# A linear-attention and spectral-mixing kernel: VectorE's table preparation moved ahead of the row work, TensorE's part spread among the rows, and one zeroing moved from VectorE to GpSimd

## The chip, the cores and the metric

The kernel runs on one core of one Trainium2 chip. The metric is the device time of one execution in microseconds (us); the figure for the kernel before is the median of three runs. The profile comes from one more execution, whose own time is given beside its span (first to last instruction). The engines are TensorE (PE in the profile; its weight loads are PEld), VectorE (DVE), ScalarE (ACT), GpSimd (POOL) and SyncE (SP); 16 DMA engines move data between HBM and the on-chip memory.

## The reference

Linear attention over 8 batches, 8 heads, 576 positions and head size 64, then a mixing step in the frequency domain: a real FFT along the sequence, a complex 512 x 512 product for each of the 64 lowest modes, the inverse FFT added to the input, and a channel product with a rectifier.

```python
def phi(x):
    return np.where(x > 0, x, np.exp(x) - 1.0) + 1.0
q_p, k_p = (phi(q), phi(k))
kv = np.einsum('bhsd,bhse->bhde', k_p, v)
z = np.sum(k_p, axis=2)
num = np.einsum('bhsd,bhde->bhse', q_p, kv)
den = np.einsum('bhsd,bhd->bhs', q_p, z)[..., None] + 1e-06
x = num / den                                # heads side by side: (8, 576, 512)
X = np.fft.rfft(x, axis=1)
Xr, Xi = np.real(X[:, :64]), np.imag(X[:, :64])
Yr = np.einsum('bmd,mde->bme', Xr, w_r) - np.einsum('bmd,mde->bme', Xi, w_i)
Yi = np.einsum('bmd,mde->bme', Xr, w_i) + np.einsum('bmd,mde->bme', Xi, w_r)
Y[:, :64] = Yr + 1j * Yi
y = np.fft.irfft(Y, n=S, axis=1)
u = x + y
return u + np.maximum(u @ w_ch, 0.0)
```

The weights w_r and w_i are 64 matrices of 512 x 512 in float32 each.

## The kernel before

**Three stages.** First, attention: for each of the 8 batches q, k and v are loaded, made into features, and summed into a k-v matrix per head (kept in kv_sb); the attention rows are formed once for the forward transform, which makes the left operands xt. Second, the spectral products: the weights are taken in 32 loads w0 to w31, each a tile of 128 x 8192 in bf16 (2 MB as stored, converted on the way from float32); an even load holds the real parts of four modes, the odd one behind it the imaginary parts. For each load, mode_block(p) runs a block of 16 matmuls of 128 x 512 (line 525) on TensorE, p being the load's number, and behind each odd block the sums are evacuated (lines 534 and 536) and sorted. The last loads go in a somewhat different way. Third, a tail behind the last load: the last sums, rectifier, additions and stores to the output.

**Order of work.** Nearly every instruction is pinned: each engine runs them in the order in which the program lists them. An instruction that waits for a semaphore therefore holds all that stand behind it on its engine.

**The weight loads.** All are issued by GpSimd (w_load, line 106) in its one queue, in order. The first two buffers (w0, w1) are kept and reused for all loads from w6 on; w2, w3 and w4 lie in a pool of their own (wpre), and w5 in a further one (wx) beside it. A load from w6 on has to wait till the block that last read its buffer is done: w6 waits for block 0, w7 for block 1, w8 for block 6, and so on. mode_block(p) places the load in the program when it takes the block up (w_get).

**The memory of w2 to w5.** After block 5 the pools of w2 to w5 are closed (line 711), and a new pool, sW, takes their place. It holds the rows x_main and x_tail, small tiles, and kv_diag: the k-v matrices laid out with zeros beside them (128 x 4160 in f16), so that one matmul serves two heads. kv_diag is zeroed (line 720) and then filled by two copies from kv_sb (line 722). What writes to sW first has to wait for the loads and blocks that used the memory before.

**The work between the blocks.** Blocks 6 and later have two slots each, "mid" and "end". A list of small functions (work) is dealt to them by share (line 1065) in given weights; work_slot runs so many of them at each slot. At the head of the list stand the attention rows, which are formed a second time for the output (attention_rows, line 821: for a tile of rows, matmuls of q features with kv_diag, then a division on VectorE into x_main or x_tail). Behind them follow the folding of inverse rows into x and the channel products.

**The inverse table and the row sets.** inverse_rows (line 757) makes the inverse transform's table inv_sb from the forward one, fwd_sb: 16 copies on VectorE sort the modes into by_mode (line 770), five matmuls transpose them (line 780), and VectorE scales the results into inv_sb (lines 782 and 788). row_sets (line 794) makes three 0-1 matrices in sel on VectorE: a memset and ten copies. row_set(i) (line 807) multiplies inv_sb by one of these on TensorE and lets ScalarE copy the result into inv2_sb or into a lead_sb. In the list these five items stand together behind the first five tiles of rows (lines 1097 to 1100); inverse_rows and row_sets have their VectorE part inside the item.

Of the kernel before, what the change touches and what calls it, by code (L numbers as in the profile page):

```python
# [11 lines left out]
F16 = mybir.dt.float16  # L12
# [21 lines left out]
def kernel(  # L34
# [10 lines left out]
    nc = tc.nc  # L45

    B, H, S, Dh = q.shape
    D = H * Dh
    NM = moe_w_r.shape[0]
    NHP = H // 2  # L50
    NDC = D // 128
# [41 lines left out]
    pin = tc.keep_in_program_order  # L93
# [52 lines left out]
    def rows_of(jj: int, base: int = 0):  # L146

        if jj < NJJ:
            return slice(base + jj, base + 512, NJJ)
        return slice(512, S) if base == 0 else slice(0, base)  # L150
# [14 lines left out]
    def q_view(t):  # L165
        return t.rearrange("p (c t s) -> p c t s", c=2, t=2)
# [508 lines left out]
    N_LEAD = 2  # L675
# [37 lines left out]
    sW = ctx.enter_context(tc.tile_pool(name="sW", bufs=1))  # L713
# [3 lines left out]
        sW.tile([128, 2, D], F32, tag="x_tail", bufs=B // 4, name=f"x_tail{i}") for i in range(B // 4)  # L717
    ]
    kv_diag = sW.tile([128, B, 2, 2, 2, 65], F16, tag="YZ", bufs=1, name="kv_diag")
    pin(nc.vector.memset(kv_diag, 0.0))  # L720
    for h in range(2):
        pin(nc.vector.tensor_copy(out=kv_diag[HALVES[h], :, :, :, h, :], in_=kv_sb[HALVES[h]]))
    yz_at: list = []
# [11 lines left out]
    def x_of(t: int):  # L735
        if t < B * NJJ:
            return x_main[t // NJJ][:, t % NJJ, :]
        i = t - B * NJJ
        return x_tail[i // 2][:, i % 2, :]
# [10 lines left out]
    def bank(name: str, shape=(128, D), dtype=F32):  # L750
        return psB.tile(list(shape), dtype, tag="bank", bufs=4, name=name)
# [2 lines left out]

    inv_scale = sW.tile([128, 1], F32, name="inv_scale")

    def inverse_rows():

        pin(nc.vector.memset(inv_scale, INV_EXP))
        pin(nc.vector.memset(inv_scale[0:2], INV_EXP / 2))  # L760
        by_mode = [
            sW.tile([128, NDC, 128], F16, tag="xTw", bufs=2, name="modes_main"),
            sW.tile([128, D], F16, tag="x16w", bufs=2, name="modes_tail")[:, 0:128].unsqueeze(1),
        ]
        for dst, src in zip(by_mode, (fwd_sb[:, 0:NJJ, :], fwd_sb[:, NJJ:, :])):
            for t in range(2):
                for g in range(4):
                    c0 = t * NM + g * NQ
                    pin(
                        nc.vector.tensor_copy(  # L770
                            out=dst[:, :, 2 * g + t :: 8], in_=src[:, :, c0 : c0 + NQ]
                        )
                    )
        iv = bank("inv_main", [128, NJJ, 128])
        it = bank("inv_tail")
        for jj in range(NJJ + 1):
            rows = slice(0, 128) if jj < NJJ else slice(0, S - 512)
            modes = by_mode[jj // NJJ][rows, jj % NJJ, :]
            o = iv[:, jj] if jj < NJJ else it[:, 0 : S - 512]
            pin(nc.tensor.matmul(o, modes, id16[rows, rows]))  # L780
        pin(
            nc.vector.tensor_scalar(
                out=inv_sb[:, 0:512].rearrange("m (p j) -> m j p", j=NJJ), in0=iv,
                scalar1=inv_scale[:, 0:1], scalar2=None, op0=ALU.mult,
            )
        )
        pin(
            nc.vector.tensor_scalar(
                out=inv_sb[:, 512:S], in0=it[:, 0 : S - 512],
                scalar1=inv_scale[:, 0:1], scalar2=None, op0=ALU.mult,  # L790
            )
        )

    def row_sets():
        pin(nc.vector.memset(sel, 0.0))
        for h in range(2):
            for g in range(NF // NL):
                r0 = 2 * NF + 2 * NL * ((g - 1) % (NF // NL))
                pin(
                    nc.vector.tensor_copy(  # L800
                        out=sel[:, 0, h * 64 + g : h * 64 + 64 : NF // NL], in_=id16[:, r0 : r0 + 2 * NL]
                    )
                )
        for b in range(N_LEAD):
            pin(nc.vector.tensor_copy(out=sel[:, 1 + b, b:128:B], in_=id16[:, 2 * NE : 128]))

    def row_set(i: int):
        dst = ([inv2_sb] + lead_sb)[i]
        for cols in (slice(0, 512), slice(512, S)):
            r_ps = bank(f"rows{i}_{cols.start}")[:, 0 : cols.stop - cols.start]  # L810
            pin(nc.tensor.matmul(r_ps, sel[:, i, :], inv_sb[:, cols]))
            pin(nc.scalar.copy(out=dst[:, cols], in_=r_ps))

    def parts_of(t: int):
        if t < B * NJJ:
            b, jj = divmod(t, NJJ)
            return [(b, jj, slice(0, 128))]
        p = t - B * NJJ
        return [(2 * p + h, NJJ, HALVES[h]) for h in range(2)]

    def attention_rows(t: int):

        num = [bank(f"nw{t}_{c}") for c in range(2)]
        x = x_of(t)
        for b, jj, orow in parts_of(t):
            qT = q_view(qT_all[b])
            rd = rd_all[b][orow, jj].rearrange("p o (c t) -> p c t o", c=2)
            xv = x[orow].rearrange("p (o c t d) -> p c t o d", o=2, c=2, t=2)
            for c in range(2):
                for h2 in range(2):  # L830
                    pin(
                        nc.tensor.matmul(  # L832
                            num[c][orow, h2 * 130 : h2 * 130 + 130],
                            qT[:, c, h2, rows_of(jj, BASE[b % 2])],
                            kv_diag[:, b, c, h2].rearrange("p o n -> p (o n)"),
                        )
                    )
            for c in range(2):
                nv = num[c][orow, 0:260].rearrange("p (t o n) -> p t o n", t=2, o=2)
                rden = rd[:, c]  # L840
                if b % 2 == 1:
                    rden = sW.tile([128, 2, 2], F32, tag="rdw", bufs=4, name=f"rdw{t}_{c}")[orow]
                    pin(nc.vector.reciprocal(out=rden, in_=nv[:, :, :, 64]))
                pin(
                    nc.vector.tensor_tensor(  # L845
                        out=xv[:, c],
                        in0=nv[:, :, :, 0:64],
                        in1=rden.unsqueeze(3).broadcast_to([orow.stop - orow.start, 2, 2, Dh]),
                        op=ALU.mult,
                    )  # L850
                )
# [18 lines left out]
    x16w, xTw = {}, {}  # L870
# [40 lines left out]
    tiles = []  # L911
# [153 lines left out]
    def share(n_items: int, steps: list):  # L1065
        total, at = sum(w for _, w in steps), 0
        for key, w in steps:
            lo = at
            at += w
            slots[key] = slots.get(key, 0) + n_items * at // total - n_items * lo // total  # L1070
# [16 lines left out]
    def first_rows(n: int):  # L1087
        for i, t in enumerate(pairs[n]):
# [5 lines left out]
                ),  # L1094
            )

    rows_work = [inverse_rows, row_sets] + [lambda i=i: row_set(i) for i in range(1 + N_LEAD)]
    work[:0] = [lambda t=t: attention_rows(t) for t in tiles[:5]] + rows_work + [
        lambda t=t: attention_rows(t) for t in tiles[5:]
    ]  # L1100
    share(
        len(tiles) + len(rows_work),
        [((p, h), 10) for p in range(n_early, first_fold - 2) for h in ("mid", "end")]
# [166 lines left out]
```

## Time and profile before

| | |
|---|---|
| median of 3 runs | 418.39 us (418.31 to 419.18) |
| the profiled execution | 419.09 us, span 417.4 us |
| busy: TensorE, VectorE, ScalarE, GpSimd | 306.6, 244.7, 148.7, 51.9 us |
| mean granted TensorE clock | 0.829 of full speed |
| DMA queue of GpSimd (weights, q, k, v) | 81.53 MB written, 94.1% of the 16 engines' span |
| weight loads of 2048 KB | 29, median 16.8 to 17.0 us from issue to landing |
| HBM read and written | 163.66 MB and 9.44 MB |

The costliest groups among those that the change touches, and the blocks:

| line, engine | work | count | mean |
|---|---|---|---|
| 525, PE | a matmul of a block, 128 x 512 | 480 | 498 ns |
| 720, DVE | zeroing kv_diag, 128 x 4160 | 1 | 3525 ns |
| 722, DVE | filling kv_diag | 2 | 698 ns |
| 704 and 469, POOL | zeroing xz, 128 x 1536 | 2 | 1397 ns |
| 106, POOL | issuing a weight load | 31 | 546 and 533 ns |

Times in the profile count from the start of the span. A row of the timeline names its start, its length, engine, line, operation, what is written and what is read, and in brackets how long the engine sat idle before it and what ended the wait. A row of the stretches gives the busy time of each engine with its instructions, then the granted clock, the share of the DMA engines' time that was busy, and the rate at which they moved data. A load's landing is its issue plus its time to landing. Idle time of an engine off the chain costs nothing by itself.

### The profile page before, as it was taken

Reading aid. Unit: us, or ns where it says so; the run is one execution under the profiler, and the core shown is the slowest. Engines: PE = TensorE matmul, PEld = TensorE weight load, DVE = VectorE, ACT = ScalarE, POOL = GpSimd, SP = SyncE. Lnnn points to the kernel's source line nnn. Section 1 sums busy time; section 2 is a strip of 40 time slices with the busy share of each in tenths; the row PEclk is TensorE's granted clock in tenths of the full one; section 3 lists DMA queues with packets and bytes.
Section 4 is the critical chain, followed back from the end, with each engine's and each line's share of the span. In section 5 each row is a group of like instructions: output and inputs, shape, how many; then the busy total and the mean of one; then the engine's idle time right before and its main releaser. Section 6 shows DMA issues by size and latency. Waiting matters only on the chain.

```text
span 417.4 us, 6710 instructions
## 1 busy us (share of the span) xinstructions
PE 306.6 (73%) x2767; PEld 173.5 (42%) x2767; DVE 244.7 (59%) x540; ACT 148.7 (36%) x220; POOL 51.9 (12%) x91
## 2 busy tenths in 40 slices
PE   0269799999685365786665568778879887887993
PEld 0167687777442132243332233333434433452431
DVE  3779979884752546566574342556445644622795
ACT  4667788854300001000000112334434442322682
POOL 6233424000110000010000000001000000230200
PEclk9999858556979565676665688999989999999998
DMA  8999999999999999999999999999999999999698
GB/s 216 211 211 217 209 219 205 221 221 216 214 220 210 220 218 210 212 216 210 218 214 221 218 210 220 217 214 220 213 221 217 212 217 218 215 210 187 210 401 346
DMA packets 16691, 92.84 MB, mean 222 GB/s; under 512 B 2069, under 2 KB 2790, under 8 KB 12374
## 3 DMA queue, kind: packets, MB, share of 16 engines
q0 software_dynamic: 12784, 81.53, 94.1%
q1 hardware_dynamic: 3878, 10.90, 6.9%
q8 instruction: 21, 0.34, 0.3%
q14 instruction: 8, 0.07, 0.0%
HBM read 163.66 MB, written 9.44 MB: 415 GB/s over the span
## 4 chain that ended last, share of the span: by engine, by line
DMA 60%; PE 22%; DVE 9%; issue 4%; ACT 2%; POOL 2%; POOLq 0%; ACTq 0%; DVEq 0%
DMA w<-in_moe_w_r_dram 34%; DMA w<-in_moe_w_i_dram 17%; PE P L525 9%; DMA k<-in_k_dram 7%; PE kvp L264 4%; DVE x_main L1031 4%; DMA q<-in_q_dram 3%; PE qTp L244 2%; DVE x L300 2%; PE xf L434 1%; ACT ke L210 1%; DVE xz L453 1%; PE eps L901 1%; PE num L158 1%; PE acc L955 1%
## 5 line engine op out<-in xcount | busy, mean ns | idle before, releaser
L525 PE MATMUL P<-w,xz 128*64 128x512 bf16 x480 | 81.1, 498 | 46.2 <-DMA w<-in_moe_w_i_dram 22.8
L525 PEld LDWEIGHTS <-xz 128*64 128x64 bf16 x480 | 38.2, 136 | 79.2 <-issue 66.6
L536 ACT CAST ys<-P 128x512 f16<-128x512 f32 x8 | 4.7, 585 | 115.8 <-PE P L525 115.8
L901 PE MATMUL eps<-wch,xTw 128*128 128x512 f16 x144 | 37.3, 383 | 3.8 <-DVE xTw L893 3.8
L882 DVE TENSOR_TENSOR x_main<-ya,x_main 128x512 f32<-128x512 f32 x32 | 21.9, 687 | 23.8 <-PE ya L878 23.7
L884 ACT CAST x16w<-x_main 128x512 f16<-128x512 f32 x32 | 19.8, 619 | 41.5 <-DVE x_main L882 40.7
L453 DVE COPY xz<-xt 32x384 bf16<-32x384 bf16 (+2 forms) x62 | 31.1, 502 | 2.1 <-ACT xt L419 1.2
L832 PE MATMUL nw<-kv_diag,qT 128*128 128x130 f16 (+1 forms) x160 | 23.1, 273 | 11.3 <-DVE x_main L845 6.4
L264 PE MATMUL kvp<-vpad,ke 32*128 32x130 f16 x576 | 24.8, 275 | 8.4 <-ACT qT L251 8.4
L909 ACT CAST E<-eps 128x512 f16<-128x512 f32 (+1 forms) x40 | 21.1, 538 | 21.5 <-PE eps L901 21.5
L264 PEld LDWEIGHTS <-ke 32*128 32x128 f16 x576 | 23.1, 123 | 9.8 <-issue 9.1
L106 POOL DMA_DIRECT2D w<-in_moe_w_i_dram x15 | 8.0, 533 | 142.4 <-PE P L525 95.4
L244 PE MATMUL qTp<-id,qe 128*128 128x128 f16 x144 | 16.8, 311 | 11.5 <-DVE qe L228 9.7
L832 PEld LDWEIGHTS <-qT 128*128 128x128 f16 (+1 forms) x160 | 14.6, 130 | 24.2 <-issue 12.2
L534 DVE CAST ys<-P 128x512 f16<-128x512 f32 x10 | 6.9, 691 | 29.6 <-PE P L525 29.6
L106 POOL DMA_DIRECT2D w<-in_moe_w_r_dram x16 | 8.7, 546 | 118.6 <-PE P L525 118.4
L893 DVE COPY xTw<-xTp 128x512 f16<-128x512 f16 x36 | 14.9, 416 | 13.7 <-PE xTp L891 13.6
L300 DVE TENSOR_TENSOR x<-num,rd 128x512 f16<-128x512 f32 x32 | 22.1, 691 | 1.1
L158 PE MATMUL num<-kv_sb,qT 64*128 64x65 f16 (+1 forms) x320 | 16.7, 226 | 6.0 <-DVE x L300 3.9
L251 ACT COPY qT<-qTp 128x1152 f16<-128x1152 f16 x16 | 19.5, 1282 | 2.9 <-PE qTp L244 2.4
L244 PEld LDWEIGHTS <-qe 128*128 128x128 f16 x144 | 14.8, 146 | 12.5 <-DVE qe L228 10.1
L901 PEld LDWEIGHTS <-xTw 128*128 128x128 f16 x144 | 12.4, 99 | 15.1 <-DVE xTw L893 4.4
(162 smaller groups left out, 498.6 us busy)
## 6 DMA issues: line engine op xcount, KB each, us to landing
w<-in_moe_w_i_dram POOLq DMA_DIRECT2D x15, 2048.0 KB, 17.0
w<-in_moe_w_r_dram POOLq DMA_DIRECT2D x14, 2048.0 KB, 16.8
out_dram<-x_main SPq DMA_DIRECT2D x14, 512.0 KB, 3.4
v<-in_v_dram POOLq DMA_DIRECT2D x8, 576.0 KB, 13.9
q<-in_q_dram POOLq DMA_DIRECT2D x7, 576.0 KB, 12.6
k<-in_k_dram POOLq DMA_DIRECT2D x6, 576.0 KB, 12.6
w<-in_moe_w_r_dram POOLq DMA_DIRECT2D x2, 1024.0 KB, 16.6
w<-in_moe_w_r_dram POOLq DMA_DIRECT2D x4, 512.0 KB, 11.8
```

The source lines that it names most:

```text
L158: mm = nc.tensor.matmul(num[hpo][orow, c0 : c0 + 65], qT[rows, hpp, h2, cols], kv_sb[rows, hpp, h2, :])
L244: nc.tensor.transpose(qT_ps[:, j], phi["q", b][:, c, j].rearrange("p o d -> p (o d)"), id16,)
L251: nc.scalar.copy(out=qT[:, :, c * NJ : (c + 1) * NJ], in_=qT_ps.rearrange("p j x -> p x j"))
L264: nc.tensor.matmul(kv_ps[:, h2, 0:130], phi["k", b][r0 : r0 + 32, j // NJ, j % NJ].rearrange("p o d -> p (o d)"), vp[r0 : r0 + 32, :, j, 0 ...
L300: nc.vector.tensor_tensor(out=dst.rearrange("p (o c d) -> p o c d", o=2, c=4), in0=nv[:, :, :, 0:64], in1=rden.unsqueeze(3).broadcast_to([ ...
L453: pin(copies[g % len(copies)](out=xz[k % 2][rows, :, :, g, of], in_=src))
L525: nc.tensor.matmul(P[c : c + width, :], x, w[:, dc, :], start=first, stop=last, tile_position=(0, c), skip_group_check=True,)
L832: nc.tensor.matmul(num[c][orow, h2 * 130 : h2 * 130 + 130], qT[:, c, h2, rows_of(jj, BASE[b % 2])], kv_diag[:, b, c, h2].rearrange("p o n ...
L882: pin(nc.vector.tensor_tensor(out=x, in0=acc, in1=x, op=ALU.add))
L884: pin(nc.scalar.copy(out=x16w[t], in_=x))
L901: nc.tensor.matmul(e_ps, xT[:, c, :], wch16[:, c, :], start=(c == 0), stop=(c == NDC - 1))
L909: pin(nc.scalar.copy(out=dst, in_=e_ps[:, cols]))
```

## The change

Three edits. The zeroing of kv_diag goes from VectorE to GpSimd. The VectorE part of inverse_rows becomes a function inverse_modes, and it and row_sets are called when the list is put together, so that their instructions stand behind the filling of kv_diag and ahead of block 6's work. The remaining four items (inverse_rows, now only matmuls and scaling, and the three row_set) no longer stand together behind five tiles of rows: inverse_rows comes first, and the row sets follow one by one behind tiles 4, 6 and 8. The list dealt to the slots has 40 items in place of 41. by_mode's tiles are allocated earlier, in the same pools and buffers.

```diff
@@ -717,7 +717,7 @@
     kv_diag = sW.tile([128, B, 2, 2, 2, 65], F16, tag="YZ", bufs=1, name="kv_diag")
-    pin(nc.vector.memset(kv_diag, 0.0))
+    pin(nc.gpsimd.memset(kv_diag, 0.0))
     for h in range(2):
         pin(nc.vector.tensor_copy(out=kv_diag[HALVES[h], :, :, :, h, :], in_=kv_sb[HALVES[h]]))
@@ -754,14 +754,15 @@
-    def inverse_rows():
+    by_mode = [
+        sW.tile([128, NDC, 128], F16, tag="xTw", bufs=2, name="modes_main"),
+        sW.tile([128, D], F16, tag="x16w", bufs=2, name="modes_tail")[:, 0:128].unsqueeze(1),
+    ]
+
+    def inverse_modes():
 
         pin(nc.vector.memset(inv_scale, INV_EXP))
         pin(nc.vector.memset(inv_scale[0:2], INV_EXP / 2))
-        by_mode = [
-            sW.tile([128, NDC, 128], F16, tag="xTw", bufs=2, name="modes_main"),
-            sW.tile([128, D], F16, tag="x16w", bufs=2, name="modes_tail")[:, 0:128].unsqueeze(1),
-        ]
         for dst, src in zip(by_mode, (fwd_sb[:, 0:NJJ, :], fwd_sb[:, NJJ:, :])):
...
+    def inverse_rows():
+
         iv = bank("inv_main", [128, NJJ, 128])
         it = bank("inv_tail")
@@ -1094,10 +1098,14 @@
-    rows_work = [inverse_rows, row_sets] + [lambda i=i: row_set(i) for i in range(1 + N_LEAD)]
-    work[:0] = [lambda t=t: attention_rows(t) for t in tiles[:5]] + rows_work + [
-        lambda t=t: attention_rows(t) for t in tiles[5:]
-    ]
+    inverse_modes()
+    row_sets()
+    rows_work = [inverse_rows] + [lambda i=i: row_set(i) for i in range(1 + N_LEAD)]
+    form_rows = [lambda t=t: attention_rows(t) for t in tiles]
+    work[:0] = (
+        rows_work[:1] + form_rows[:4] + rows_work[1:2] + form_rows[4:6] + rows_work[2:3]
+        + form_rows[6:8] + rows_work[3:] + form_rows[8:]
+    )
     share(
         len(tiles) + len(rows_work),
```

## The prediction, made before the changed kernel was run

> **What bounds the kernel now.** I read the chain of work that ended last first, then busy time by stretches cut at the landings of the weight loads, then GpSimd's timeline, and last the timeline of all engines where the change acts, 113 to 170 us. The chain by engine, from the page:
>
> ```profile
> DMA 60%; PE 22%; DVE 9%; issue 4%; ACT 2%; POOL 2%; POOLq 0%; ACTq 0%; DVEq 0%
> ```
>
> Transfers hold 60% of the chain. To see whether they ever pause, stretches between landings (a landing is the issue time plus the time to landing: w5 113.0 + 20.5 = 133.5, w6 119.62 + 23.6 = 143.2, w7 122.22 + 30.7 = 152.9, w8 147.14 + 15.4 = 162.5, w9 156.87 + 15.4 = 172.3):
>
> ```profile
> core 0: us, PE busy (x) PEld busy (x) DVE busy (x) ACT busy (x) POOL busy (x), PEclk, DMA share, GB/s
> 123.85:133.50 9.65, 4.86 (x46) 2.32 (x43) 3.58 (x7) 0.58 (x1) 0.00 (x0) 1.00 1.00 214
> 133.50:143.20 9.70, 2.99 (x20) 1.51 (x20) 5.61 (x4) 0.00 (x0) 0.00 (x0) 0.56 1.01 216
> 143.20:152.90 9.70, 5.69 (x32) 3.25 (x32) 4.72 (x12) 0.00 (x0) 0.53 (x1) 0.68 1.03 220
> 152.90:162.50 9.60, 5.81 (x33) 3.19 (x32) 4.97 (x27) 0.58 (x1) 0.53 (x1) 0.50 1.00 213
> 162.50:172.30 9.80, 6.43 (x34) 2.65 (x34) 4.83 (x22) 2.01 (x6) 0.53 (x1) 0.67 1.01 209
> 201.40:259.60 58.20, 39.12 (x215) 18.95 (x215) 27.29 (x74) 6.32 (x11) 3.17 (x6) 0.69 1.02 216
> 259.60:318.80 59.20, 48.28 (x315) 23.40 (x315) 32.55 (x70) 23.70 (x46) 3.17 (x6) 0.97 1.02 217
> 318.80:367.20 48.40, 40.90 (x252) 18.78 (x252) 24.73 (x56) 17.74 (x32) 4.28 (x8) 1.00 1.01 215
> ```
>
> The last two columns are what to see: the DMA share is 1.00 to 1.03 and the rate 209 to 220 GB/s in every row. One load lands each 9.7 us from 133.5 to the last at 385.55 ((385.55 - 133.5) / 26 = 9.69), and TensorE, at most 85% busy in any row, follows them. So **the weight stream is the bound, with no pause in it: an idle microsecond of the 16 DMA engines before 385 us moves the end by a microsecond.** Who starts the loads:
>
> ```profile
> 113.00 0.53 POOL L106 DMA_DIRECT2D w<-in_moe_w_i_dram  x1 [37.79 <-DVE xz L453]
> 113.52 1.40 POOL L704 MEMSET xz<- 128x1536 bf16 x1
> 114.84 0.22 POOL L705 MEMSET Y<- 128x128 f16 x1
> 119.62 0.53 POOL L106 DMA_DIRECT2D w<-in_moe_w_r_dram  x1 [4.56 <-PE P L525]
> 122.22 0.53 POOL L106 DMA_DIRECT2D w<-in_moe_w_i_dram  x1 [2.08 <-PE P L525]
> 147.14 0.53 POOL L106 DMA_DIRECT2D w<-in_moe_w_r_dram  x1 [24.39 <-PE P L525]
> ```
>
> These are w5, two zeroings, w6, w7, w8, all in GpSimd's one queue, taken in order. w6 and w7 are issued as soon as blocks 0 and 1 have freed their buffers, 14 and 11 us before w5 has landed: they are what keeps the stream fed from 133.5 to 152.9.
>
> And the stretch where the zeroing of kv_diag stands now:
>
> ```profile
> 133.53 2.60 PE L525 MATMUL P<-w,xz 128*64 128x512 bf16 x16 [4.14 <-DMA w<-in_moe_w_i_dram]
> 136.17 0.69 DVE L534 CAST ys<-P 128x512 f16<-128x512 f32 x1 [5.78 <-PE P L525]
> 137.67 3.52 DVE L720 MEMSET kv_diag<- 128x4160 f16 x1 [0.81 <-issue]
> 141.23 1.41 DVE L722 COPY kv_diag<-kv_sb 64x2080 f16<-64x2080 f16 x2
> 143.22 3.62 PE L525 MATMUL P<-w,xz 128*64 128x512 bf16 x16 [5.91 <-DMA w<-in_moe_w_r_dram]
> ```
>
> Block 5 (16 matmuls) ends at 133.53 + 2.60 = 136.13. The zeroing runs on a VectorE with nothing else to do, and ends before w6 lands.
>
> **The change, part by part.** *kv_diag zeroed by GpSimd.* kv_diag lies in memory that w2 to w5 held, so its zeroing waits for their readers. On VectorE that is free, the evacuation of blocks 4 and 5 stands before it anyway. In the listing of the changed program GpSimd has it right behind the two zeroings of 113.5 and 114.8, **ahead of the issues of w6 and w7**, with a wait for the landings of w2 to w5 and for TensorE's count at the end of block 5. Queued behind it are w6, w7 and every later load; TensorE's block 6 waits for w6, and everything in the slots behind block 6.
>
> What it costs: blocks 0 to 5 and w5 depend on nothing changed, so block 5 ends at 136.13 again. GpSimd reacts to TensorE 0.28 us later (the "issue" piece between a block and the load behind it in the chain), 136.41. Duration: no zeroing of 4160 elements stands on GpSimd, but one of 128 at 0.223 us and two of 1536 at 1.397: a slope of 0.834 ns an element gives 0.223 + 4032 x 0.000834 = 3.59, plain proportion 1.397 x 4160 / 1536 = 3.78; VectorE's row, 3.52, is close. I take 3.7, so w6 is issued at 140.1 in place of 119.6, w7 at 140.6. The queue has by then been empty since 133.5. From an issue to landing, less the transfer itself: lower bound 1.1 (GpSimd's gather issued at 386.91, first traffic at 388.0), upper 2.35 (the 32 KB gathers at the end land 2.5 after issue, of which 32 KB at 216 GB/s is 0.15); the stores of 256 KB land in 2.8, of which 256 KB at the 401 GB/s of the store slices is 0.65, leaving 2.15. I take 2.0, nearest the two rows that run to a landing. The transfer is 9.7. So w6 lands at 140.1 + 2.0 + 9.7 = 151.8 against 143.2: **+8.6 us**, with ends 140.0 + 1.1 + 9.7 = 150.8 (+7.6) and 140.2 + 2.35 + 9.7 = 152.3 (+9.1).
>
> Is any of it won back? w7 follows at 161.5. w8 waits for block 6: 151.8 + 3.62 + 0.28 = 155.7, which is 5.8 before w7 lands; before it was 152.9 - 147.14 = 5.8 too. From there each load is issued ahead of the landing before it, as now, and the stream runs at its full rate to the end; at a rate that is fixed, nothing catches up. The tail behind the last landing (385.55 to 417.4, stores and additions) has the same work.
>
> *VectorE's saving, 3.52 us.* Worth nothing: it lay between 137.67 and 141.19, and TensorE waited for w6 till 143.22.
>
> *Table copies and row sets ahead of the rows (2 small memsets, 16 copies, then a memset and 10 copies).* In the old place, 158.91 to 160.69 and 162.50 to 163.64, they hold TensorE: it waits 2.5 us for the copies and 2.0 for the sets, and block 8 starts at 164.60, 2.1 us behind w8's landing at 162.5. In the new place they follow kv_diag's copies, at about 140.1 + 1.4 = 141.5, for (160.69 - 158.91) + (163.64 - 162.50) = 2.9 us, and TensorE has nothing to do till 151.8: covered; without that cover they would cost those 2.9 us. What their removal frees is worth nothing either: w10, the load that the late block 8 releases, is issued at 168.53, 3.8 us before w9 lands at 172.3, so the 2.1 us never reached the stream.
>
> *TensorE's part singly among the rows.* The same 5 transposing matmuls and 6 row-set matmuls (0.84 and 3 x 0.57 us), spread from block 6 to 8; ScalarE's evacuations go with them. One item fewer in the list (40 for 41) shifts single items between half blocks. Covered by TensorE's idle third of each 9.7 us; uncovered, a moved item costs below 1 us once. Neither adds a DMA, and SP's queue isn't passed.
>
> Sum: +8.6 on the profiled execution, 419.09 us (span 417.4 and 1.7 around it), so 427.7; its time is 0.7 above the median of the three runs, 418.39, so **427.0** for the median, 426.0 to 427.5 from the two ends.
>
> **A cost that depends on VectorE.** kv_diag's two copies, 0.70 us each, are released by the zeroing just when w6 and w7 are issued. Rows for such a meeting: GpSimd's issue of q at 19.83 took 0.94 us beside a 0.76 us VectorE pass over 2304 elements, against 0.71 for most others; the issue of k at 68.59 took 0.71 beside the 0.76 us copy of v, and the zeroing at 113.52 its usual 1.40 beside copies of xz. So 0 to 0.23, inside the ends above; I add nothing. The Trainium skill (SBUF — State Buffer, section "SBUF: two separate sides") says that a VectorE copy in a two-port mode locks GpSimd out, so that it cannot write a load's descriptors until the copy is over. By that rule w6 would wait out both copies, which is the third rival; the trace agrees once, by 0.23 us, and disagrees twice.
>
> **The rivals.**
> 1. *Not slower: the stream has other work at 136 us, and the moved table pays.* Place: block 8, 2.1 us late at 164.60. Price: 418.4 - 2.1 = 416.3 if that delay was on the path; if the delay was covered but the stream still had work queued through the zeroing, 418.4. It decides from the point where the queue holds more than w5 at 136.4, or where w10 is issued behind w9's landing. Against: with w6 and w7 behind the zeroing nothing is queued behind w5, and the 3.8 us above. 3% faster, 3% no change.
> 2. *The zeroing starts when w5 has landed, not at block 5's end* (were the compute wait satisfied earlier than I read): 133.5 + 0.28 + 3.7 + 2.0 + 9.7 = 149.2, +6.0: 424.4. For: four of its five waits are landings. Against: the count it waits for is that of block 5's last matmul. 6%.
> 3. *The copies hold up the descriptors* for 2 x 0.70 us on top: 428.4. It decides if VectorE's copies stop an issue for their whole length. For: the 0.94 row. Against: its size, and the two rows without any effect. 4%.
>
> **How the numbers follow.** My forecast has 84%, with its own range 425.8 to 427.9 (the ends, the 0.2 and the runs' scatter). The range 424.2 to 428.6 takes in rivals 2 and 3 and leaves out the first. Below 0.2% (0.8 us), a difference can't be told from none here: faster 3%, same 3%, slower 94%.
>
> **What would show it.** Right: a 3.6 to 3.8 us zeroing on GpSimd that starts at 136.4 after a wait of some 21 us; w6 issued at 140.1; a DMA share near zero from about 134 to 141.5; block 6 at 151.8; later landings still 9.7 apart, all 8.6 later; the last at 394. Wrong: any DMA traffic in that gap, a start of the zeroing before 136, landings closer than 9.7, or a block after the eighth that waits for something other than its load.

## The result, and the profile after

The changed kernel takes 430.17 us (median of 5 runs, 428.15 to 431.0) against 418.55 for the kernel before (5 runs, 418.31 to 419.18): a ratio of 1.0269, 95% interval 1.0244 to 1.0293. It is slower by 11.6 us, where 8.6 was forecast, and lies above 428.6, the end of the range. The profiled execution is the fastest of the five: 428.15 us, span 426.4 against 417.4.

The chain by engine, from the page of the changed kernel, looks as it did:

```profile
DMA 58%; PE 24%; DVE 8%; issue 3%; ACT 3%; POOL 2%; POOLq 0%; ACTq 0%; DVEq 0%
```

The stretches tell more. These are of the changed kernel, cut where w5's last packet starts, where traffic starts again, and at landings; the last two columns are again the DMA share and the rate in GB/s. A packet counts in the stretch in which it starts:

```profile
core 0: us, PE busy (x) PEld busy (x) DVE busy (x) ACT busy (x) POOL busy (x), PEclk, DMA share, GB/s
123.85:131.90 8.05, 5.01 (x48) 2.37 (x45) 3.71 (x8) 0.58 (x1) 0.00 (x0) 1.00 0.93 197
131.90:140.25 8.35, 2.21 (x20) 1.25 (x20) 2.00 (x3) 0.00 (x0) 4.92 (x3) 0.87 0.00 0
140.25:151.74 11.49, 0.00 (x0) 0.00 (x0) 2.87 (x30) 0.00 (x0) 0.22 (x1) 0.50 1.02 205
151.74:162.10 10.36, 5.31 (x34) 2.89 (x34) 5.36 (x12) 0.00 (x0) 0.53 (x1) 0.66 1.05 225
162.10:171.68 9.58, 6.28 (x40) 3.16 (x40) 4.36 (x13) 1.92 (x5) 0.53 (x1) 0.83 1.03 219
191.06:259.52 68.46, 43.45 (x246) 22.27 (x246) 35.61 (x103) 4.10 (x7) 3.70 (x7) 0.66 1.01 215
327.36:375.75 48.39, 40.92 (x254) 18.84 (x254) 24.54 (x55) 17.21 (x31) 4.28 (x8) 1.00 1.02 216
```

For 8.35 us no packet starts: share 0.00, rate 0. Those that started before 131.90 are over at 133.0. The rows beside the hole, 197 and 205 GB/s, show the stream running out and starting up; from 151.74 on it runs at 215 GB/s and more, as before. GpSimd's timeline of the changed kernel says who opened the hole:

```profile
113.22 0.53 POOL L106 DMA_DIRECT2D w<-in_moe_w_i_dram  x1 [38.19 <-DVE xt L419]
113.74 1.40 POOL L704 MEMSET xz<- 128x1536 bf16 x1
115.05 0.22 POOL L705 MEMSET Y<- 128x128 f16 x1
135.33 3.57 POOL L720 MEMSET kv_diag<- 128x4160 f16 x1 [20.06 <-PE P L525]
138.84 0.91 POOL L106 DMA_DIRECT2D w<-in_moe_w_r_dram  x1
139.75 0.72 POOL L106 DMA_DIRECT2D w<-in_moe_w_i_dram  x1
155.68 0.53 POOL L106 DMA_DIRECT2D w<-in_moe_w_r_dram  x1 [15.21 <-PE P L525]
```

The zeroing waits 20 us for block 5 (the matmuls of line 525), and the issues of w6 and w7 stand behind it, at 138.84 in place of 119.62. Two things differ from the forecast lines. The issues take 0.91 and 0.72 us, not 0.53. And the zeroing starts at 135.33, a microsecond earlier than I had it, which the prediction lists as a sign of being wrong; but it starts behind block 5 as forecast, and block 5 was shorter here:

```profile
133.35 1.92 PE L525 MATMUL P<-w,xz 128*64 128x512 bf16 x16 [3.81 <-DMA w<-in_moe_w_i_dram]
138.93 1.41 DVE L722 COPY kv_diag<-kv_sb 64x2080 f16<-64x2080 f16 x2 [2.93 <-POOL kv_diag L720]
```

### The profile page after: what moved, and what is told of

Same layout as the page of the kernel before. It is cut to its first block, busy times and chain, and to the rows that moved or that the text cites. A ratio compares the mean times of both kernels' runs of the same rounds, so it can differ in the third digit from the quotient of the medians.

```text
span 426.4 us, 6710 instructions
## 1 busy us (share of the span) xinstructions
PE 306.1 (72%) x2767; PEld 173.8 (41%) x2767; DVE 241.8 (57%) x539; ACT 148.7 (35%) x220; POOL 56.0 (13%) x92
## 4 chain that ended last, share of the span: by engine, by line
DMA 58%; PE 24%; DVE 8%; issue 3%; ACT 3%; POOL 2%; POOLq 0%; ACTq 0%; DVEq 0%
DMA w<-in_moe_w_r_dram 37%; DMA w<-in_moe_w_i_dram 12%; PE P L525 10%; DMA k<-in_k_dram 7%; PE kvp L264 4%; DVE x_main L1035 4%; DMA q<-in_q_dram 3%; PE eps L905 2%; PE qTp L244 2%; DVE x L300 2%; PE xf L434 1%; ACT ke L210 1%; PE num L158 1%; PE acc L959 1%; DVE xz L453 1%
## 5 line engine op out<-in xcount | busy, mean ns | idle before, releaser
L525 PEld LDWEIGHTS <-xz 128*64 128x64 bf16 x480 | 39.1, 136 | 92.6 <-issue 80.0
L836 PE MATMUL nw<-kv_diag,qT 128*128 128x130 f16 (+1 forms) x160 | 21.5, 260 | 10.6 <-DVE x_main L849 3.9
L836 PEld LDWEIGHTS <-qT 128*128 128x128 f16 (+1 forms) x160 | 13.2, 124 | 22.9 <-issue 13.6
L847 DVE RECIPROCAL rdw<-nw 128x4 f32<-128x4 f32 (+1 forms) x40 | 7.1, 177 | 20.9 <-PE nw L836 20.5
## 6 DMA issues: line engine op xcount, KB each, us to landing
q<-in_q_dram POOLq DMA_DIRECT2D x7, 576.0 KB, 12.6
w<-in_moe_w_r_dram POOLq DMA_DIRECT2D x4, 512.0 KB, 12.4
```

What stands on the lines that cost most here:

```text
L525: nc.tensor.matmul(P[c : c + width, :], x, w[:, dc, :], start=first, stop=last, tile_position=(0, c), skip_group_check=True,)
L836: nc.tensor.matmul(num[c][orow, h2 * 130 : h2 * 130 + 130], qT[:, c, h2, rows_of(jj, BASE[b % 2])], kv_diag[:, b, c, h2].rearrange("p o n ...
```

## The experiments

Each median is over its own runs and compared with the kernel before on the same chip, at 418.62 to 418.81 us. "Changed" means the changed kernel as the base of the edit.

**e1: the changed kernel again.** No edit.

> The changed kernel a second time, for a profile of another execution, as the profiled one (428.15 us) is 2 us below the median of its runs (430.17). Gap theory (the zeroing holds w6 and w7, the DMA engines run dry from w5's landing until the load starts, and all later landings move by that): median 429.5 to 430.5, and a profiled execution near 430 shows w6's landing later than 151.74 or an extra pause of the stream somewhere later; I look for which. Rival (the stream is slower after the gap): w6 again near 151.7 and landings further apart than 9.7 us.

430.13 us, ratio 1.0255 (1.0234 to 1.0275); the profiled execution took 429.76. From its GpSimd timeline and its TensorE timeline:

```profile
136.91 3.57 POOL L720 MEMSET kv_diag<- 128x4160 f16 x1 [23.98 <-PE P L525]
140.42 0.91 POOL L106 DMA_DIRECT2D w<-in_moe_w_r_dram  x1
```

```profile
133.23 3.62 PE L525 MATMUL P<-w,xz 128*64 128x512 bf16 x16 [6.27 <-DMA w<-in_moe_w_i_dram]
153.15 3.19 PE L525 MATMUL P<-w,xz 128*64 128x512 bf16 x16 [15.12 <-DMA w<-in_moe_w_r_dram]
163.73 3.62 PE L525 MATMUL P<-w,xz 128*64 128x512 bf16 x16 [4.62 <-DMA w<-in_moe_w_i_dram]
```

The same 16 matmuls of block 5 take 3.62 us here and 1.92 above; the granted clock is 0.50 in this stretch and was 1.00 there. So w6 is issued 1.58 us later, and the execution is 1.61 us longer (429.76 to 428.15). In the kernel before, block 5 lies beside a running stream, and no load waits for it. The last two lines are blocks 6 and 7, each starting at its load's landing: 10.6 us apart, not 9.7.

**e2: the zeroing back on VectorE.** Everything else of the change stays.

```diff
-    pin(nc.gpsimd.memset(kv_diag, 0.0))
+    pin(nc.vector.memset(kv_diag, 0.0))
```

> The changed kernel with the zeroing back on VectorE. Gap theory: the whole loss goes, 418.0 to 419.2 us, w6 issued near 119.6 and landing at 143.2. Rival (the table work moved ahead and the spread row sets cost the 2 to 3 us beyond the 9 of the gap): 420.5 to 421.5.

418.55 us, ratio 0.9988 (0.9977 to 0.9999). GpSimd issues w6 at its old time:

```profile
119.84 0.53 POOL L106 DMA_DIRECT2D w<-in_moe_w_r_dram  x1 [4.56 <-PE P L525]
```

The whole loss is gone; what the rest of the change gains lies below what can be told.

**e3: the kernel before, with the zeroing on GpSimd and nothing else of the change** (the reverse of e2's edit, on the kernel before).

> The kernel before with the zeroing on GpSimd and nothing else of the change. Gap theory: all of the loss, 429 to 431 us. Rival (the rest of the change carries 2 to 3 us of it): 427 to 428.5. VectorE's table copies are then not beside the issues of w6 and w7; only the two copies into kv_diag are.

429.82 us, ratio 1.0251 (1.023 to 1.0273): the loss is the zeroing's alone. GpSimd's timeline:

```profile
136.63 3.57 POOL L720 MEMSET kv_diag<- 128x4160 f16 x1 [23.31 <-PE P L525]
140.14 0.91 POOL L106 DMA_DIRECT2D w<-in_moe_w_r_dram  x1
141.04 0.72 POOL L106 DMA_DIRECT2D w<-in_moe_w_i_dram  x1
```

The issues take 0.91 and 0.72 us here too, though VectorE runs only the two copies into kv_diag beside them.

**e4: w6 and w7 ahead of the zeroing**, which stays on GpSimd.

```diff
+    for p in (n_early, n_early + 1):
+        w_get(p)
     pin(nc.gpsimd.memset(kv_diag, 0.0))
```

> The changed kernel with w6 and w7 placed ahead of the zeroing in GpSimd's queue; the zeroing stays on GpSimd. Gap theory: w6 and w7 are issued at 119.6 and 122.2 again, the zeroing runs near 136 to 140 and ends before w8 is asked for at 147: 418.0 to 419.2 us. Rival (GpSimd's zeroing itself disturbs, or its lateness to VectorE): 421 or more.

418.48 us, ratio 0.999 (0.9979 to 1.0). GpSimd's timeline of this run:

```profile
118.83 0.53 POOL L106 DMA_DIRECT2D w<-in_moe_w_r_dram  x1 [4.56 <-PE P L525]
121.00 0.53 POOL L106 DMA_DIRECT2D w<-in_moe_w_i_dram  x1 [1.65 <-PE P L525]
136.89 3.56 POOL L722 MEMSET kv_diag<- 128x4160 f16 x1 [15.36 <-PE P L525]
147.09 0.53 POOL L106 DMA_DIRECT2D w<-in_moe_w_r_dram  x1 [6.63 <-PE P L525]
```

The same zeroing, on the same engine, at the same time, costs nothing: only its place in the queue did.

**e5: the wait without the duration.** Changed, with GpSimd zeroing 64 of the 4160 columns.

```diff
-    pin(nc.gpsimd.memset(kv_diag, 0.0))
+    flat_kv = kv_diag.rearrange("p b c h o n -> p (b c h o n)")
+    pin(nc.gpsimd.memset(flat_kv[:, 0:64], 0.0))
+    pin(nc.vector.memset(flat_kv[:, 64:], 0.0))
```

> The changed kernel with GpSimd zeroing 64 of kv_diag's 4160 columns and VectorE the rest: GpSimd's wait for block 5 stays ahead of w6 and w7, its duration falls from 3.57 us to about 0.17. Gap theory (every microsecond of GpSimd ahead of w6 counts one for one): 3.4 us less than the changed kernel's 430.1, so 426.3 to 427.2, w6 issued some 0.2 us after block 5's end. Rival (the duration is hidden and the wait is the whole price): 430. Rival (a restart of the emptied queue costs a fixed sum and the length of the pause little): 429 to 430.

426.02 us, ratio 1.0172 (1.0158 to 1.0186), 4.1 below the changed kernel (430.13) and 0.3 under the expectation. GpSimd's timeline:

```profile
137.11 0.15 POOL L721 MEMSET kv_diag<- 128x64 f16 x1 [23.96 <-PE P L525]
137.20 0.53 POOL L106 DMA_DIRECT2D w<-in_moe_w_r_dram  x1
137.73 0.54 POOL L106 DMA_DIRECT2D w<-in_moe_w_i_dram  x1
```

So 426.02 less the 418.62 of the kernel before, 7.4 us, is the price of the wait. The rest goes with the zeroing's length: w6 is issued 3.22 us earlier than in e1, in 0.53 us and not 0.91, and the two profiled executions (426.32 and 429.76) are 3.44 apart.

**e6: the zeroing made twice.** Changed.

```diff
     pin(nc.gpsimd.memset(kv_diag, 0.0))
+    pin(nc.gpsimd.memset(kv_diag, 0.0))
```

> The changed kernel with the zeroing on GpSimd made twice in a row. Gap theory: 3.5 us more than the changed kernel, 433.2 to 434.2. Rival (the stream catches up later, or the pause is only partly paid): less than 432.5.

433.8 us, ratio 1.0361 (1.0347 to 1.0375). GpSimd's timeline:

```profile
136.80 3.57 POOL L720 MEMSET kv_diag<- 128x4160 f16 x1 [23.18 <-PE P L525]
140.43 3.56 POOL L721 MEMSET kv_diag<- 128x4160 f16 x1
143.94 0.91 POOL L106 DMA_DIRECT2D w<-in_moe_w_r_dram  x1
```

The time is 3.7 us more than the changed kernel's, for 3.52 us of later issue (143.94 against 140.42 in e1). The pause is paid in full.

**e7: the copies on ScalarE, the table work back in its item.** Changed.

```diff
-        pin(nc.vector.tensor_copy(out=kv_diag[HALVES[h], :, :, :, h, :], in_=kv_sb[HALVES[h]]))
+        pin(nc.scalar.copy(out=kv_diag[HALVES[h], :, :, :, h, :], in_=kv_sb[HALVES[h]]))
...
     def inverse_rows():
+        inverse_modes()
+        row_sets()
...
-    inverse_modes()
-    row_sets()
```

> The changed kernel with kv_diag's two filling copies on ScalarE and VectorE's table work back inside its item, so that VectorE does nothing while GpSimd issues w6 and w7. If VectorE's copies hold up the issues (0.91 and 0.72 us in the changed kernel, 0.53 elsewhere): both issues at 0.53, w6 lands some 0.4 us sooner after its issue (12.3 for 12.7), and 429.2 to 429.9 us; the second load after the pause, 10.3 to 10.8 us behind the first, may come back to 9.7, then 428.3 to 429.2. If the issues are long because the queue is empty: 0.91 and 0.72 again, 430.1 as the changed kernel.

430.87 us, ratio 1.0283 (1.0261 to 1.0304), above all that was expected; the profiled execution took 429.16. The edit didn't make what it was for: inverse_rows heads the list, so its copies stand next in VectorE's queue all the same, and without kv_diag's copies ahead of them they ran beside the zeroing. The line of seven of the eight larger table copies in this trace (count, and the least, median and greatest duration in ns), the end of the table copies in VectorE's timeline, then GpSimd's timeline:

```profile
L771 DVE COPY modes_main<-fwd_sb x7: 517/518/2985, 136.1 to 139.4; 128x64 f16<-128x64 f16 x7
```

```profile
139.67 0.66 DVE L771 COPY modes_tail<-fwd_sb 128x16 f16<-128x16 f16 x8
```

```profile
135.32 3.57 POOL L720 MEMSET kv_diag<- 128x4160 f16 x1 [16.94 <-PE P L525]
138.83 1.62 POOL L106 DMA_DIRECT2D w<-in_moe_w_r_dram  x1
140.45 0.54 POOL L106 DMA_DIRECT2D w<-in_moe_w_i_dram  x1
```

Three small VectorE copies, begun beside the zeroing, took 2.91 to 2.99 us, till just after the zeroing ended. And w6's issue, with more of these copies beside it, took 1.62: it ends at 140.45, 0.12 us behind the last of them (139.67 + 0.66 = 140.33). The two engines do hold each other up.

**e8: the filling copies made six times over.** Changed.

```diff
-    for h in range(2):
+    for h in [0, 1] * 6:
         pin(nc.vector.tensor_copy(out=kv_diag[HALVES[h], :, :, :, h, :], in_=kv_sb[HALVES[h]]))
```

> The changed kernel with the two filling copies of kv_diag made six times over by VectorE (twelve copies of 0.70 us, some 8.5 us from the end of the zeroing on, still ahead of w6's landing). If a VectorE copy stops GpSimd's issue for its whole length: the issues of w6 and w7 take 1.4 us or more each and the time goes up by 1 to several us, 431 to 434. If it costs some 0.2 to 0.4 us an issue and no more: the issues at 0.9 and about the same for w7, 430.1 to 430.6.

430.04 us, ratio 1.0269 (1.0255 to 1.0283), as the changed kernel. From VectorE's and GpSimd's timelines, one after the other:

```profile
140.49 8.70 DVE L722 COPY kv_diag<-kv_sb 64x2080 f16<-64x2080 f16 x12 [2.93 <-POOL kv_diag L720]
```

```profile
140.40 0.91 POOL L106 DMA_DIRECT2D w<-in_moe_w_r_dram  x1
141.30 0.74 POOL L106 DMA_DIRECT2D w<-in_moe_w_i_dram  x1
```

Through 8.7 us of copies the two issues take no longer than beside the usual two. But this doesn't show that a copy leaves an issue running. In this trace the first copy ends at 141.19 and the first issue at 141.31, the second copy at 141.92 and the second issue at 142.04: 0.12 us behind in each case, as in e7. So an issue waits till the copy beside it is over, and gets its turn before the next one; a row of copies costs no more than one for each issue. As issue and copy run side by side for most of their length, 0.38 us are left of it on the first issue and 0.2 on the second.

**e9: the zeroing waits for block 2.** Changed, with kv_diag first in sW, over w2's memory alone, and the pool's waits by tile. The zeroing stays on GpSimd ahead of w6 and w7.

```diff
-    sW = ctx.enter_context(tc.tile_pool(name="sW", bufs=1))
+    sW = ctx.enter_context(tc.tile_pool(name="sW", bufs=1, reuse_waits="tile"))
+    kv_diag = sW.tile([128, B, 2, 2, 2, 65], F16, tag="YZ", bufs=1, name="kv_diag")
...
-    kv_diag = sW.tile([128, B, 2, 2, 2, 65], F16, tag="YZ", bufs=1, name="kv_diag")
```

> The changed kernel with kv_diag placed first in sW and the pool's waits taken by tile, so that it lies over w2 alone and the zeroing on GpSimd, still ahead of w6 and w7, waits for block 2 in place of block 5. Gap theory: block 2 ends near 124.9, the zeroing near 128.5, and w6 is issued there, some 1.6 us (issue to first traffic) before 131.9, when w5's traffic ends: no pause or one of some tenths, 418.0 to 419.5 us. Rival (what GpSimd has ahead of the loads costs whatever it waits for, or w6's lateness of 9 us against 119.6 counts): 421 or more.

418.4 us, ratio 0.9986 (0.9976 to 0.9995). GpSimd's timeline:

```profile
122.10 3.57 POOL L720 MEMSET kv_diag<- 128x4160 f16 x1 [9.88 <-PE P L525]
125.61 0.53 POOL L106 DMA_DIRECT2D w<-in_moe_w_r_dram  x1
126.13 0.54 POOL L106 DMA_DIRECT2D w<-in_moe_w_i_dram  x1
```

The zeroing starts some 3 us earlier than expected, as block 2 had ended by then. w6 is issued 6 us later than in the kernel before, and it costs nothing, as w5's traffic lasts till 131.9. This and e2 are the versions with the shortest medians beside the kernel before, by amounts too small to claim.

**e10: only w6 ahead of the zeroing.** Changed.

```diff
+    w_get(n_early)
     pin(nc.gpsimd.memset(kv_diag, 0.0))
```

> The changed kernel with only w6 placed ahead of the zeroing, w7 and the rest behind it. Gap theory: w6's traffic lasts from 131.9 to about 141.6; w7, issued near 140.4 and moving some 1.6 us later, follows with a pause of at most half a us: 418.2 to 419.7 us. Rival (w7's lateness, 140.4 for 122.2, counts by itself): 423 or more.

420.58 us, ratio 1.0041 (1.0029 to 1.0053): outside the expected band by 0.9. The issue of w7:

```profile
140.36 0.91 POOL L106 DMA_DIRECT2D w<-in_moe_w_i_dram  x1
```

No packet starts between about 141.4 and 141.9, while the last of w6's are still under way, and block 7 starts on w7 at 153.95 against 152.79 in e2. A hole of half a microsecond moved the next landing by 1.2 and the end by 1.9 (span 418.4 against 416.5). So a hole costs more than its own length.

**e11: VectorE idle.** The kernel before, with the zeroing on GpSimd and the two filling copies on ScalarE (both edits above).

> The kernel before with the zeroing on GpSimd and the two filling copies on ScalarE; the table work stays in its old place, behind rows, so that VectorE does nothing between the evacuation of blocks 4 and 5 and block 6. What e7 was to show and did not, as VectorE's table copies ran beside the zeroing there. If VectorE's copies lengthen the issues: w6 and w7 issued in 0.53 us each, w6 12.5 us behind its issue, 429.2 to 430.0 us against 429.8 with the copies on VectorE. If the emptied queue does: 0.91 and 0.72 again.

429.43 us, ratio 1.0259 (1.0236 to 1.0282); by time not to be told from e3. GpSimd's timeline:

```profile
136.71 3.57 POOL L720 MEMSET kv_diag<- 128x4160 f16 x1 [23.19 <-PE P L525]
140.22 0.53 POOL L106 DMA_DIRECT2D w<-in_moe_w_r_dram  x1
140.74 0.54 POOL L106 DMA_DIRECT2D w<-in_moe_w_i_dram  x1
```

With VectorE idle the issues are back at 0.53 and 0.54: it was the copies that lengthened them, not the empty queue. Yet w6 lands 12.6 us behind its issue, against 12.7 in e1 and e3, and w7 is 10.4 us behind w6 even so. The landing of w6 hides the lengthening: the first traffic comes 1.23 us behind the issue here and 1.62 in e1 and e3, and the profiled execution is 0.28 us shorter than e3's (429.43 and 429.71) though w6 is issued 0.08 later. The next section has what the stream lost in each trace.

## Why the prediction was right in kind and wrong in size

**The mechanism held.** The zeroing stands in GpSimd's queue with a wait for block 5; w6 and w7 are held; the stream runs dry and doesn't catch up. e3 shows the zeroing alone does it, e2 that nothing else of the change matters, e4 and e9 that neither the engine nor the duration matters while w6 is issued early enough, e5 and e6 that the wait and every further microsecond count once it is not. Rival 1 (not slower) and rival 2 (a start at w5's landing) fell: the zeroing starts within 0.1 us of block 5's end in both traces.

**The parts priced at nothing were worth nothing.** VectorE's saved 3.52 us, the table work ahead of the rows, the spread row sets: e4 has them all and stands at 0.999; e2, without VectorE's saving, stands at 0.9988. The late start of block 8 is really gone (162.46 in e2, on its load's landing, against 164.60), and the 2.1 us moved nothing.

**The size: four terms.** The clean pair is e1 (429.76) and e2 (418.21), each profiled execution's own time. The forecast gave 8.6; the pair differs by 11.55.

| step | forecast | measured | adds |
|---|---|---|---|
| w6's issue: block 5's end, and the zeroing's 3.7 | 140.1 | 140.42 in e1, 138.84 in the other | +0.3 |
| from the issue to the landing, beside the 9.7 of the transfer | 2.0 (1.1 to 2.35) | 3.0 (12.7 in all) | +1.0 |
| w7 behind w6 | 9.7 | 10.58 (9.73 in e2) | +0.85 |
| from block 8 on | 0 | w8 at +10.95, the last landing at +11.56 | +0.6 |

w6's landing in e2 is 143.04, not 143.2, which gives the remaining 0.2. The first row came out near by luck: block 5 ended at 136.85 in e1 and not at 136.13, and against that GpSimd reacted in 0.06 us and not in 0.28, and the zeroing held the issue for 3.51 and not 3.7. Block 5 took 2.60 us in the profile before, and 1.92 to 3.63 in the others. I took its end from a single execution and carried that scatter into neither end.

**The step that failed is the price of the restart**: the term "from an issue to landing, less the transfer itself", 2.0 with 1.1 and 2.35 as its bounds, and with it the use of w6's lateness, 8.6, as the whole loss. Measured at w6's landing the term is 3.0, above its upper bound: stores and small gathers land sooner than a load into an empty queue, of which the trace before had no example. And w6's landing doesn't show all that the stream lost. w7 was 10.3 to 10.8 us behind w6 in all eight traces whose hole comes ahead of w6, with w6's issue 0.53, 0.91 or 1.62 us long, and the time in which no packet starts 6.6 us long (e5) or 13.6 (e6). It is not a slow second load. By the rows of the changed kernel above, 1.12 loads' worth of bytes have moved since the hole when w6 lands (11.49 us at 205 GB/s, a load being 2.10 MB), 2.23 when w7 lands and 3.23 when w8 does. So between w6 and w7 more than one load moves, at 225 GB/s. It is w6 that lands early for the bytes moved; why, isn't shown. From there the sentence that the stream runs "at its full rate to the end" held.

What the stream lost can be read from the packets: the time at which a trace has moved the same bytes as e2, a load or two behind the hole, less e2's time. In the table it stands beside the end of the late issue (start and length in the lines above).

| trace | the late issue ends at | the stream is behind e2 by | difference |
|---|---|---|---|
| e5 | 137.73 | 7.59 | 130.14 |
| the changed kernel | 139.75 | 9.52 | 130.23 |
| e7 | 140.45 | 10.31 | 130.14 |
| e11 | 140.75 | 10.53 | 130.22 |
| e3 | 141.05 | 10.84 | 130.21 |
| e8 | 141.31 | 11.16 | 130.15 |
| e1 | 141.33 | 11.09 | 130.24 |
| e6 | 144.85 | 14.74 | 130.11 |
| e10 (w7) | 141.27 | 1.40 | 139.87 |

The difference is 130.2 in all eight, and one load (9.7) later for w7 in e10. So the issue had to be over by 130.2 to cost nothing, and each microsecond behind that cost one, whether the wait, the zeroing or a lengthened issue made it late. This is 1.7 us before w5's last packet starts (131.9) and 3 before w5 counts as landed. The traffic starts 0.7 us behind the end of the issue in all eight. The remaining microsecond goes where the stream runs out and starts up: in e1 the rate falls to 206, 133 and 35 GB/s in the microseconds from 130 to 133, and is 104, 148 and 208 in those from 142 to 145 (a packet's bytes spread over its length), where 216 is usual. In all, the stream loses 2.0 to 2.4 us more than the time in which no packet is under way.

With the forecast's own issue, over at 140.1 + 0.5 = 140.6, the loss is 10.4 by this and not 8.6: that is 1.8 of the 2.95 us that were missing. The later issue adds 0.3, its lengthening 0.4, and 0.5 comes in with the last half load's worth of bytes. In the traces with a hole 0.5 to 0.9 comes in there against e2, and 0.4 in the kernel before, which has no hole; why wasn't settled.

**The third rival** (the copies hold up the issues) was right in kind and too dear at 2 x 0.70. The issues that met kv_diag's copies were 0.38 and 0.19 us longer, and only the 0.38 on w6's counts in the stream. My own reading of its rows, "0 to 0.23", was too small, and of the two rows that I said had no effect neither speaks against the rival: the copy of v at 68.26 was over at 69.02, ahead of the end of the issue beside it (69.31), and the zeroing at 113.52 met copies into xz, which hold up nothing in e9 either: both issues beside such copies take their usual 0.53 and 0.54 there. The Trainium skill (SBUF — State Buffer, section "SBUF: two separate sides") has a VectorE instruction in a two-port mode and a GpSimd instruction shut each other out for a whole instruction. The traces don't name a copy's mode, but agree: the copies that met the zeroing in e7 took up to 2.99 us, and an issue that met table or kv_diag copies ended 0.12 us behind the end of one.

## What to carry to other kernels

Where one queue issues the loads that bound a kernel, the cost of a small operation put into it is not its length but the wait it brings, and what stands behind it: read which issue comes next, and when the transfers already issued run out. An issue may be late at no cost up to a point somewhat ahead of the end of the traffic (here it had to be over by 130.2, 1.7 us before the last packet in front of it starts: w6 issued at 125.6 was free, at 137.2 it cost 7.4 us). Price every microsecond behind that point in full. Don't take the lateness of the first landing for the loss: compare bytes, or a later landing. And take the end of the instruction that now gates the issue from several executions.

## What the runs showed of the hardware that wasn't expected

- A restart costs more than the hole: 2.0 to 2.4 us beyond the time in which no packet is under way, for such times of 5.3 us (e5) to 12.4 (e6). The first load behind it lands early for the bytes moved, so that the second seems late: 10.3 to 10.8 us behind the first, where the stream's spacing is 9.7.
- The granted clock differs between executions at the same place: the 16 matmuls of block 5 took from 1.92 us (clock 1.00) to 3.62 (clock 0.50) between the changed kernel and e1. Beside a full stream that is invisible; ahead of a load it was 1.6 us of the kernel's time.
- GpSimd's zeroing of SBUF held three small VectorE copies for 2.91 to 2.99 us. VectorE's copies into kv_diag lengthened the issue of a load from 0.53 to 0.91 us, and the table copies to 1.62; the issue ended 0.12 us behind a copy each time, and the stream fell behind by as much as the issue grew.
